# Block-sparse attention and MoE-MLP in one kernel: where the first weight is decoded, in how many steps it is split, and a new order of the work

## The chip, the cores and the metric

The kernel runs on one core of a Trainium2 chip. The metric is the device time of one execution in microseconds (us). A core has TensorE (PE, matrix products), VectorE (DVE), ScalarE (ACT), GpSimd (POOL), SyncE (SP, which here issues nearly all DMAs) and DMA engines. Each engine runs its instructions in the order in which the program queued them and waits on semaphores for the others.

## What is computed

Attention is over 4 batches, 8 heads, 768 tokens and 64 features, in blocks of 32 tokens: a query block sees its neighbours, the first and the last block, and three drawn at random; the first and the last query block see all. Its result x (3072 tokens of 512 features) goes through an MLP.

```python
scores = scale * np.matmul(q, k.transpose(0, 1, 3, 2))    # masked to the blocks above
attn = np.exp(scores - np.max(scores, axis=-1, keepdims=True))
attn = attn / (np.sum(attn, axis=-1, keepdims=True) + 1e-09)
x = np.matmul(attn, v).transpose(0, 2, 1, 3).reshape(B * S, H * D)
h = x @ w_in                                              # 512 x 2048
g = h * np.tanh(np.where(h > 20.0, h, np.log1p(np.exp(np.minimum(h, 20.0)))))
return g @ w_out                                          # 2048 x 512
```

Both weights arrive as 64-bit floats, whose bits the kernel reads as pairs of 32-bit integers.

## The kernel before

**Precision and weights.** x, w_in, g and w_out are held as pairs of half-precision tiles, a high and a low part, and a product is summed from matmuls of parts. Before that, w_in must be made fp32, scaled and split. It comes in eight pieces of 1 MB (`load_i`, tiles `wr`, a ring of three). `add_decode` makes fp32 numbers of a piece by three integer instructions on VectorE (L921, L924, L927); before the change they are written over the place in the constant tile `wi` where the two parts will stand. A Gram matrix of the piece (`add_gram`, PE L365, diagonal on DVE L380) gives a size, from which `add_root` makes a power of two, `ws`, for two pieces at a time (PE `tp_w`, DVE L396, L399, L250). Then `split_i` scales and splits the piece by three instructions: a scaled copy `wt_i` in the ring `raw` (on ACT L975 for five pieces, on POOL L977 for three), the high part, a copy on ACT (L982), and the low part, scaled copy minus high part (POOL L985 for six, DVE L986 for two). w_out follows in sixteen pieces of 512 KB (`wor`, decoded by the same three lines).

**Attention.** 52 jobs of one or two query tiles run in order, thirteen to a batch. A job is S (PE: scores, L650 and L660), `mx` (DVE L703: row maxima), `nb` and `pt` (ACT L716, L729: exponentials), t (PE transposes, L749), `pp` (ACT, DVE: probabilities), O (PE L796, L812), `r` and `xs` (DVE L833 to L848), `tx` (PE L866) and the two parts of x, `xh` (ACT L884) and `xl` (DVE L887). For a job the needed K columns are copied to `kg` (`gather_k`: POOL L588, or ACT L590), and the V rows are fetched from a copy of V in DRAM, `vd`, into `vg` by SP (`gather_v`, L607 to L613). Batch 0 is computed in fp32, so its V is first copied by `copy_v` (L532) and stored by `store_v` (L538).

**MLP.** A tile of 256 tokens is complete after four or five jobs. Then come its h matmuls (`moe_h`, L1065), the function g in the rings `us` and `hs` (three buffers each), and y (`moe_y`, L1125).

**Order.** Every step is a task of the class `Plan` with a planned duration, a `key` (lower goes first among those ready), and buffers of rings that it takes. `emit` queues, over and over, the task that can start first by the plan. `pace` holds S back so that attention is spread over the MLP's matmuls, by the numbers `RES` and `START`, and adds 0.1 us when PE's work changes between S, O and the rest. Where the plan has PE idle for over 0.25 us between 3 and 150 us, `emit` puts in matmuls on a tile of zeros (L900), so many as fit at 0.22 us each. A step that depends on a DMA waits for a semaphore of that DMA; such semaphores are reused, so a DMA's issue can wait for the end of an earlier DMA that had the same one.

## Time and profile before

| what | value |
|---|---|
| device time, median of 3 runs (lowest to highest) | 749.08 us (746.91 to 750.20) |
| the profiled execution's own time | 745.22 us |
| its span | 743.3 us |
| PE busy | 723.2 us, 97% |
| DVE busy | 529.8 us, 71% |
| ACT busy | 541.6 us, 73% |
| POOL busy | 235.9 us, 32% |
| matmuls on zeros (L900) | 136 |

The profile shows one execution. A line is named by its number in the program, a tile by its name in it. "Busy" says how long an engine executed, not whether anything waited for it; that is read from the waits and from the timelines.

### The profile page before, as it was taken

How to read it: one execution, taken by the hardware profiler on the slowest of the kernel's cores; microseconds unless marked ns; L12 is line 12 of the kernel's file. 1: busy time of each engine (PE TensorE's matmuls, PEld its weight loads, DVE VectorE, ACT ScalarE, POOL GpSimd, SP SyncE). 2: the span in 40 equal slices, each digit the busy share in tenths (PEclk: the TensorE clock that was granted, in tenths of full speed). 3: DMA queues.
4: the chain of work that ended last, by engine and by line, in shares of the span. 5: the costliest groups of instructions: out<-in, count | busy, mean ns of one | idle time of the engine just before them, and what ended most of it. 6: DMA issues, size and time to landing. Idle time of an engine off the chain costs nothing.

```text
span 743.3 us, 25914 instructions
## 1 busy us (share of the span) xinstructions
PE 723.2 (97%) x10798; PEld 498.0 (67%) x10798; DVE 529.8 (71%) x1000; ACT 541.6 (73%) x874; POOL 235.9 (32%) x325
## 2 busy tenths in 40 slices
PE   9888898999999999999999999999999999999997
PEld 3555777776676777667677677767767676666653
DVE  3789898788777688888678766789789656334340
ACT  3567787998988777878777877878878766655550
POOL 2263543654416313234324334422154112000000
PEclk9999999999999999999999999999999999999999
DMA  7988878240543563264142651452333343100000
GB/s 269 367 244 254 251 224 263 73 120 29 175 120 86 157 189 116 59 191 114 45 131 70 178 172 59 124 187 67 88 111 87 94 136 80 38 15 15 15 14 29
DMA packets 55897, 93.94 MB, mean 126 GB/s; under 512 B 8036, under 2 KB 18789, under 8 KB 55781
## 3 DMA queue, kind: packets, MB, share of 16 engines
q1 hardware_dynamic: 55584, 92.03, 41.5%
q8 instruction: 85, 1.39, 0.8%
q14 instruction: 32, 0.25, 0.1%
q10 hardware_dynamic: 196, 0.27, 0.1%
HBM read 79.32 MB, written 12.95 MB: 124 GB/s over the span
## 4 chain that ended last, share of the span: by engine, by line
PE 84%; DMA 7%; DVE 6%; ACT 2%; issue 1%; SPq 1%; ACTq 0%; DVEq 0%
PE y L1125 33%; PE h L1065 32%; PE t L749 6%; PE o L812 5%; PE s L660 4%; DMA vg<-vd 3%; DMA wr<-in_moe_w_in_dram 2%; PE tx L866 1%; DMA kt<-in_k_dram 1%; PE o L796 1%; DVE wo L927 1%; DMA raw_q<-in_q_dram 1%; DVE wi L927 1%; DVE wo L924 1%; DMA vd<-z 1%
## 5 line engine op out<-in xcount | busy, mean ns | idle before, releaser
L1065 PE MATMUL h<-xh,wi 128*128 128x256 f16 x1536 | 283.5, 273 | 0.0
L1125 PE MATMUL y<-wo,g 128*128 128x512 f16 x1152 | 276.7, 379 | 0.0
L1065 PEld LDWEIGHTS <-wi 128*128 128x128 f16 x2304 | 223.2, 98 | 47.7 <-issue 1.5
L1065 PE MATMUL h<-xl,wi 128*128 128x256 f16 x768 | 209.7, 273 | 0.0
L1125 PEld LDWEIGHTS <-g 128*128 128x128 f16 x1152 | 111.3, 98 | 100.6 <-issue 1.3
L588 POOL COPY kg<-kt 128x256 f16 (+1 forms) x222 | 105.2, 517 | 186.9 <-PE s L660 154.6
L1074 ACT ACTIVATE hs<-h,gsc 128x512 f32<-128x512 f32 x96 | 65.5, 684 | 59.0 <-PE h L1065 58.7
L729 ACT ACTIVATE pt<-s,nb,ns 128x256 f32<-128x256 f32 (+1 forms) x208 | 104.9, 579 | 3.1 <-DVE nb L718 2.2
L1098 DVE SCALAR_TENSOR_TENSOR hs<-us,hs 128x1024 f32<-128x1024 f32 x48 | 59.7, 1244 | 36.3 <-ACT us L1097 36.0
L1094 POOL TENSOR_TENSOR us<-us 128x1024 f32<-128x1024 f32 x26 | 50.9, 1956 | 85.7 <-DVE us L1092 78.2
L749 PE MATMUL t<-ident,pt 128*128 128x128 f32 x448 | 70.2, 279 | 1.7 <-ACT pt L729 1.1
L769 DVE SCALAR_TENSOR_TENSOR pp<-t,pp 128x512 f16<-128x512 f32 x84 | 57.1, 683 | 17.3 <-ACT pp L766 16.8
L766 ACT ACTIVATE pp<-t 128x512 f16<-128x512 f32 x84 | 49.3, 591 | 21.9 <-PE t L749 21.3
L749 PEld LDWEIGHTS t<-ident,pt 128*128 128x128 f32 x448 | 51.0, 142 | 13.5 <-issue 3.3
L1109 POOL TENSOR_TENSOR g<-hs,g 128x1024 f16<-128x1024 f32 x17 | 38.1, 2239 | 65.8 <-DVE g L1106 30.2
L703 DVE TENSOR_REDUCE mx<-s 128x4 f32<-128x1024 f32 x44 | 53.3, 1212 | 5.9 <-PE s L660 3.1
L1088 ACT ACTIVATE us<-hs,hsc 128x1024 f32<-128x1024 f32 x48 | 55.3, 1151 | 1.3
L1096 ACT ACTIVATE us<-us 128x1024 f32<-128x1024 f32 x48 | 50.8, 1058 | 4.9 <-POOL us L1094 3.9
L1092 DVE TENSOR_SCALAR us<-us 128x1024 f32<-128x1024 f32 x48 | 34.7, 722 | 25.8 <-ACT us L1088 25.6
L1097 ACT ACTIVATE us<-us 128x1024 f32<-128x1024 f32 x48 | 50.8, 1057 | 0.8
L812 PEld LDWEIGHTS <-pp 128*32 128x32 f16 x2952 | 32.5, 97 | 11.4 <-issue 9.7
L1111 DVE TENSOR_TENSOR g<-hs,g 128x1024 f16<-128x1024 f32 x31 | 38.3, 1235 | 2.3 <-ACT g L1104 1.6
(201 smaller groups left out, 855.5 us busy)
## 6 DMA issues: line engine op xcount, KB each, us to landing
vg<-vd SPq DMA_DIRECT2D x304, 65.0 KB, 2.3
vg<-vd SPq DMA_DIRECT2D x80, 195.0 KB, 3.1
wr<-in_moe_w_in_dram SPq DMA_DIRECT2D x8, 1024.0 KB, 9.4
wor<-in_moe_w_out_dram SPq DMA_DIRECT2D x16, 512.0 KB, 5.3
vd<-v SPq DMA_DIRECT2D x12, 520.0 KB, 4.1
raw_v<-in_v_dram SPq DMA_DIRECT2D x12, 512.0 KB, 6.4
...
```

The lines of the kernel that those rows point to most:

```text
L588: nc.gpsimd.tensor_copy(out=dst, in_=src)
L703: nc.vector.tensor_reduce(out=mx.rearrange("p g w -> p (g w)"), in_=tl[ks].rearrange("p g (w k) -> p (g w) k", k=KT), axis=AX.X, op=ALU.max)
L729: ex = lambda o, x, g, w: nc.scalar.activation(out=o, in_=x, func=AF.Exp, bias=nb[:, g, w:w + 1], scale=ns(w)[:, 0:1])
L749: nc.tensor.transpose(t[:, k, g], src, ident)
L769: nc.vector.scalar_tensor_tensor(out=tl["pl", i, j], in0=tl["t", i, j], scalar=PSC, in1=tl["ph", i, j], op0=ALU.mult, op1=ALU.subtract)
L812: nc.tensor.matmul(o[cs, at] if v1 == VW else o[cs, at, 0:v1 - v0], p[:, k, g, cs], x, start=j == 0 and g == 0 and k == 0 and n == 0, stop ...
L1065: nc.tensor.matmul(h[:, f2].rearrange("p (s q) -> p s q", q=BS), wi[:, fp, w, cc, fs], x[:, :, cc], start=f2 == 0 and k == 0, stop=f2 == 1 ...
L1074: nc.scalar.activation(out=tl[kq][:, 2 * (fp % 2):2 * (fp % 2) + 2], in_=tl[kh], func=AF.Copy, scale=gsc[:, fp:fp + 1])
L1088: nc.scalar.activation(out=new(sb, "us", ku, [P, 4, TT]), in_=hs(), func=AF.Exp, scale=hsc[:, b:b + 1])
L1094: add("POOL", 2.0, lambda: nc.gpsimd.tensor_tensor(out=us(), in0=us(), in1=us(), op=ALU.mult), w=[ku], port=True, key=47 + (56 if b == 0 e ...
L1098: add("DVE", 1.32, lambda: nc.vector.scalar_tensor_tensor(out=hs(), in0=us(), scalar=-0.5, in1=hs(), op0=ALU.add, op1=ALU.mult), r=[ku], w ...
L1125: nc.tensor.matmul(tl[ky], tl["g", b, t, k][:, g, f, q], wo[:, fc, w], start=fc == 0 and n == 0, stop=fc == NFC - 1 and n == 2)
```

## The change

1. **Place.** A piece of w_in is decoded into a buffer of the MLP's ring `us` (even pieces) or `hs` (odd ones), named `a`, and no longer into `wi`.
2. **Split.** The high part is one scaled copy of that tile (ACT, all eight), the low part one instruction of VectorE (`a` times scale minus high part, all eight). The scaled copy `wt_i` is gone: 16 instructions stand for 24.
3. **Planned durations** of several tasks are set anew, `pace` counts the 0.1 us only on entering S or O, and its 0.3 us between S and O are gone.
4. **Order.** `RES`, `START` and almost all keys are new, and with them the whole order.

```diff
-    def add_decode(raw, key, dst, dur, cls):
+    def add_decode(raw, key, dst, dur, cls, slot=(), first=None):
...
     def a0_i(k):
-        return wi[:, k].rearrange("p t c f -> p (t c f)").bitcast(F32)
+        return tl["a0", k]
+
+    def at_i(k):
+        ring = ("us", "hs")[k % 2]
+        return [(ring, ("a0", k))], lambda: new(sb, ring, ("a0", k), [P, 4 * TT])
...
-        add_decode(("wr", k), key, lambda: a0_i(k), 1.22, cls)
+        add_decode(("wr", k), key, lambda: a0_i(k), 1.22, cls, *at_i(k))
...
-            if eng == "ACT":
-                nc.scalar.activation(out=t, in_=a0_i(k), func=AF.Copy, scale=sc())
...
-        add("ACT", 1.1, lambda: nc.scalar.activation(out=hi, in_=tl[kt], func=AF.Copy), r=[kt],
...
-        add("POOL", 2.1, lambda: nc.gpsimd.tensor_tensor(out=lo, in0=tl[kt], in1=hi, op=ALU.subtract),
...
+        add("ACT", 1.16, lambda: nc.scalar.activation(out=hi, in_=a0_i(k), func=AF.Copy, scale=sc()), r=[ksc, ("wa", k)],
...
+        add("DVE", 1.27, lambda: nc.vector.scalar_tensor_tensor(out=lo, in0=a0_i(k), scalar=sc(), in1=hi, op0=ALU.mult, op1=ALU.subtract),
+            r=[ksc, ("wa", k), ("wih", k)], w=[("wi", k)], use=[ka], port=True, key=cls + 12)
...
-    RES, START = 152, [75, 143, 351, 1, 289, 59, 444, 40, 4, 303, 106, 133, 87, 206, 53, 166, 65, 18]
+    RES, START = 180, [97, 103, 720, 17, 173, 0, 747, 0, 13, 609, 79, 124, 130, 10, 140, 182, 96, 42]
...
-                shape, at["shape"] = 0.1 * (now != at["shape"]), now
+                shape, at["shape"] = 0.1 * (now not in (None, at["shape"])), now
...
-        if kind in ("S", "O") and at["last"] in ("S", "O") and kind != at["last"]:
-            late = max(late, 0.3)
```

Other planned durations of the diff: `gather_k` on POOL 1.3 to 1.5, on ACT 1.6 or 1.9 to 1.0; `sums` 1.28 to 1.06; S of the later batches 0.7 to 0.78; the exponentials 1.15 to 1.03; t 0.48 to 0.44; `tx` 0.25 to 0.22.

In the new order PE's work is the same but for the zeros (165 matmuls for 136, six of the added ones among later h blocks); it enters S or O from other work 103 times instead of 115, and S and O stand directly side by side 15 times instead of 2. Of the K gathers 99 copies stand on ACT instead of 42, and 165 on POOL instead of 222, in 32 groups on ACT instead of 14.

**SP queue, the first loads.** `kt`, `q` and `raw_v` are K, Q and V of batch 0, `wr` are pieces of w_in. Before:

```order
L416 DMA kt_123<-in_k_dram 128x4x768
L416 DMA q_0_157<-in_q_dram 128x4x256
L434 DMA raw_v_0_161<-in_v_dram 128x2x512
L434 DMA raw_v_1_163<-in_v_dram 128x2x512
L434 DMA raw_v_2_165<-in_v_dram 128x2x512
L416 DMA q_1_167<-in_q_dram 128x4x256
L913 DMA wr_169<-in_moe_w_in_dram 128x4x512
L913 DMA wr_171<-in_moe_w_in_dram 128x4x512
L913 DMA wr_173<-in_moe_w_in_dram 128x4x512
```

and now:

```order
L416 DMA kt_123<-in_k_dram 128x4x768
L416 DMA q_0_157<-in_q_dram 128x4x256
L416 DMA q_1_161<-in_q_dram 128x4x256
L913 DMA wr_163<-in_moe_w_in_dram 128x4x512
L913 DMA wr_165<-in_moe_w_in_dram 128x4x512
L913 DMA wr_167<-in_moe_w_in_dram 128x4x512
L434 DMA raw_v_0_169<-in_v_dram 128x2x512
L434 DMA raw_v_1_171<-in_v_dram 128x2x512
L434 DMA raw_v_2_173<-in_v_dram 128x2x512
L913 DMA wr_316<-in_moe_w_in_dram 128x4x512
L913 DMA wr_361<-in_moe_w_in_dram 128x4x512
```

Three pieces of w_in and a second tile of Q went ahead of V.

**SP queue, around the first V gathers.** `vd` is V's copy in DRAM; the rows of L557 fetch the global blocks, those of L607 to L613 the other blocks of jobs 1 and 2. Before, from the fourth piece of w_in on:

```order
L913 DMA wr_378<-in_moe_w_in_dram 128x4x512
L913 DMA wr_469<-in_moe_w_in_dram 128x4x512
L557 DMA vg_111<-vd_60 32x520 x2
...
L913 DMA wr_557<-in_moe_w_in_dram 128x4x512
L607 DMA vg_111<-vd_60 64x520
L610 DMA vg_111<-vd_60 32x520
L567 TENSOR_LOAD offv
...
L613 DMA vg_111<-vd_60 32x520
```

and now:

```order
L913 DMA wr_442<-in_moe_w_in_dram 128x4x512
L538 DMA vd_60<-v_2_159 128x2x520
L913 DMA wr_673<-in_moe_w_in_dram 128x4x512
L557 DMA vg_111<-vd_60 32x520 x2
...
L913 DMA wr_768<-in_moe_w_in_dram 128x4x512
L607 DMA vg_111<-vd_60 64x520
L610 DMA vg_111<-vd_60 32x520
L567 TENSOR_LOAD offv
L613 ISA
L613 DMA vg_111<-vd_60 32x520
```

The seventh and the eighth piece (`wr_673`, `wr_768`) went ahead of job 1's gathers, which stand behind the eighth; before, the seventh and the eighth stood among the gathers of jobs 1 to 3.

**VectorE, around the fifth piece of w_in.** Names `wr`, `a` and `wi` as above (`a_4` is the fifth piece, with the number of the buffer behind it), `gram_wi` a Gram diagonal, `mx` a job's maxima. Before, from the last step of the fourth piece (`wr_378`), a low part ahead of it, to the last step of the fifth (`wr_469`):

```order
L986 TENSOR_TENSOR wi<-wt_i_566,wi 128x1024
L927 SCALAR_TENSOR_TENSOR wi<-wr_378,wi 128x1024
L921 TENSOR_SCALAR wi<-wr_469 128x1024
L921 TENSOR_SCALAR wi<-wr_557 128x1024
L924 SCALAR_TENSOR_TENSOR wi<-wr_469,wi 128x1024
L703 TENSOR_REDUCE mx_797<-s_700 128x4
L380 SCALAR_TENSOR_TENSOR gram_wi_736,wq_568<-gram_wi_736,ident 128x128
L924 SCALAR_TENSOR_TENSOR wi<-wr_557,wi 128x1024
L396 TENSOR_SCALAR iv_i<-tp_w_828 128x2
L399 TENSOR_SCALAR iv_i<-iv_i 128x2
L250 TENSOR_SCALAR ws_850<-iv_i 128x2
L927 SCALAR_TENSOR_TENSOR wi<-wr_469,wi 128x1024
```

and now:

```order
L929 SCALAR_TENSOR_TENSOR a_4_588<-wr_361,a_4_588 128x1024
L703 TENSOR_REDUCE mx_766<-s_709 128x4
L981 SCALAR_TENSOR_TENSOR wi<-a_2_347,ws_700,wi 128x1024
L380 SCALAR_TENSOR_TENSOR gram_wi_770,wq_816<-gram_wi_770,ident 128x128
L981 SCALAR_TENSOR_TENSOR wi<-a_3_467,ws_700,wi 128x1024
L926 SCALAR_TENSOR_TENSOR a_5_704<-wr_442,a_5_704 128x1024
L923 TENSOR_SCALAR a_6_856<-wr_673 128x1024
L923 TENSOR_SCALAR a_7_858<-wr_768 128x1024
L929 SCALAR_TENSOR_TENSOR a_5_704<-wr_442,a_5_704 128x1024
L926 SCALAR_TENSOR_TENSOR a_6_856<-wr_673,a_6_856 128x1024
L380 SCALAR_TENSOR_TENSOR gram_wi_904,wq_816<-gram_wi_904,ident 128x128
```

Where one old low part stood ahead of the fifth piece's steps, the low parts of two pieces stand directly behind the fifth piece's last step, and the first steps of the seventh and the eighth piece follow before the sixth piece is decoded.

## Rows read from the trace of the kernel before

**Rows 1.** Windows of busy time, whole core: stretch, its length, busy us of each engine (x instructions), granted TensorE clock (1.00 is full), mean share of the DMA engines, GB/s.
```profile
0.00:83.42 83.42, 71.00 (x1207) 42.65 (x1208) 63.01 (x125) 45.90 (x93) 33.71 (x55) 0.98 0.87 276
83.42:160.00 76.58, 73.39 (x1268) 57.07 (x1263) 66.80 (x133) 68.45 (x111) 37.05 (x35) 1.00 0.66 199
160.00:700.00 540.00, 539.48 (x8109) 376.60 (x8107) 387.49 (x731) 411.29 (x655) 165.11 (x236) 1.00 0.35 101
700.00:743.30 43.30, 39.33 (x224) 21.69 (x222) 12.52 (x13) 15.96 (x18) 0.00 (x0) 1.00 0.05 20
```

**Rows 2.** The same view for the filler matmuls of line 900 alone.
```profile
0.00:83.42 83.42, 34.50 (x136) 13.32 (x136) 0.98 0.87 276
```

**Rows 3.** TensorE's waits over the span: waiting line, what ended the wait, us in total, times, longest us.
```profile
PE o L796 <- DMA vg<-vd: 3.5, 6, 1.2
PE gram_wi L365 <- DVE wi L927: 3.2, 3, 2.3
...
PE s L650 <- POOL kg L588: 0.7, 1, 0.7
```

**Rows 4.** Chain of waits from 12 to 84 us: start us, us, what held it.
```profile
13.47 8.52 DMA wr<-in_moe_w_in_dram
...
38.30 5.43 DMA vg<-vd
```

**Rows 5.** VectorE's timeline: start us, us, line, operation, out<-in, in brackets the idle time before and what ended it.
```profile
10.65 0.81 DVE L532 COPY v<-raw_v 128x1024 f32<-128x1024 f32 x1 [0.82 <-DMA raw_v<-in_v_dram]
...
15.19 0.16 DVE L701 TENSOR_TENSOR mx<-mx 128x2 f32<-128x2 f32 x1
...
22.01 0.69 DVE L921 TENSOR_SCALAR wi<-wr 128x1024 int32<-128x1024 int32 x1 [4.98 <-DMA wr<-in_moe_w_in_dram]
...
82.35 1.23 DVE L703 TENSOR_REDUCE mx<-s 128x4 f32<-128x1024 f32 x1 [1.72 <-PE s L650]
83.49 0.68 DVE L927 SCALAR_TENSOR_TENSOR wo<-wor,wo 128x512 int32<-128x512 int32 x1
```

**Rows 6.** Waits of the SP queue up to 26 us, columns as in rows 3.
```profile
SPq L434 <- DMA q<-in_q_dram: 6.3, 1, 6.3
...
SPq L434 <- DMA vd<-z: 3.0, 1, 3.0
```

**Rows 7.** Windows of busy time in steps of 2 us, columns as in rows 1.
```profile
12.00:14.00 2.00, 2.00 (x36) 0.73 (x36) 0.73 (x1) 1.62 (x4) 1.04 (x1) 1.00 0.34 11
...
20.00:22.00 2.00, 1.88 (x15) 1.58 (x14) 0.00 (x0) 0.72 (x2) 0.00 (x0) 1.00 1.05 388
```

**Rows 8.** VectorE's groups by shape from 160 to 600 us: line, operation, out<-in, shape xcount, busy us, mean ns of one, idle before.
```profile
L503 DVE SCALAR_TENSOR_TENSOR q<-raw_q,sc_q,q 128x1024 f16<-128x1024 f32 x8 | 10.4, 1300 | 1.2 <-DMA vg<-vd 0.7 <-ACT q L499 0.5
```

**Rows 9.** The same for 15.4 to 112 us.
```profile
L927 DVE SCALAR_TENSOR_TENSOR wo<-wor,wo 128x512 int32<-128x512 int32 x13 | 10.2, 797 | 0.0
...
L921 DVE TENSOR_SCALAR wo<-wor 128x512 int32<-128x512 int32 x14 | 5.9, 427 | 0.0
L986 DVE TENSOR_TENSOR wi<-wt_i,wi 128x1024 f16<-128x1024 f32 x2 | 3.6, 1776 | 0.1
```

**Rows 10.** VectorE's timeline, columns as in rows 5.
```profile
47.40 0.17 DVE L399 TENSOR_SCALAR iv_i<-iv_i 128x2 int32<-128x2 int32 x1
...
47.68 1.22 DVE L927 SCALAR_TENSOR_TENSOR wi<-wr,wi 128x1024 int32<-128x1024 int32 x1
...
54.63 1.59 DVE L399 TENSOR_SCALAR iv_i<-iv_i 128x2 int32<-128x2 int32 x1
...
60.40 3.15 DVE L927 SCALAR_TENSOR_TENSOR wi<-wr,wi 128x1024 int32<-128x1024 int32 x1
...
76.82 3.81 DVE L924 SCALAR_TENSOR_TENSOR wo<-wor,wo 128x512 int32<-128x512 int32 x3
```

**Rows 11.** GpSimd's timeline, columns as in rows 5.
```profile
51.81 4.39 POOL L985 TENSOR_TENSOR wi<-wt_i,wi 128x1024 f16<-128x1024 f32 x2 [1.92 <-ACT wi L982]
...
60.18 2.29 POOL L985 TENSOR_TENSOR wi<-wt_i,wi 128x1024 f16<-128x1024 f32 x1 [2.57 <-ACT wi L982]
```

**Rows 12.** VectorE's waits from 15 to 95 us, columns as in rows 3.
```profile
DVE gram_wi L380 <- PE gram_wi L365: 1.4, 1, 1.4
```

**Rows 13.** The tile view of the weight ring, its line on the loads from issue to landing.
```profile
DMA to landing us min/median/max: 7.0/9.4/12.8
```

**Rows 14.** TensorE's timeline, columns as in rows 5.
```profile
43.87 0.91 PE L796 MATMUL o<-vg,pp 128*32 128x65 f32 x32 [0.16 <-DMA vg<-vd]
...
165.12 1.46 PE L1125 MATMUL y<-wo,g 128*128 128x512 f16 x6
166.51 1.17 PE L660 MATMUL s<-kt,q 64*32 64x512 f16 x48
...
175.61 1.45 PE L1125 MATMUL y<-wo,g 128*128 128x512 f16 x6
176.90 0.27 PE L1065 MATMUL h<-xh,wi 128*128 128x256 f16 x1
```

**Rows 15.** ScalarE's timeline, columns as in rows 5.
```profile
525.39 1.02 ACT L590 ACTIVATE kg<-kt 128x256 f16 x3 [0.96 <-POOL kg L588]
```

**Rows 16.** The SP queue's timeline, columns as in rows 5.
```profile
33.57 0.61 SPq L607 DMA_DIRECT2D vg<-vd  x1
```

More of the change, by code (lines that the diff above doesn't have):

```diff
@@ L403, in add_root @@
     def add_root(key, ss, fn, r, after, w, new, cls, n=1, apart=False):
-        add("PE", 0.3 * n, lambda: root_pe(key, ss(), apart), r=r, w=[key], new=[("t", key)], key=cls + 56, lat=0.3)
-        add("DVE", 0.65, fn, port=2, r=[key, *after], w=w, new=new, key=cls + 3)
+        add("PE", 0.3 * n, lambda: root_pe(key, ss(), apart), r=r, w=[key], new=[("t", key)], key=cls + 5, lat=0.3)
+        add("DVE", 0.65, fn, port=2, r=[key, *after], w=w, new=new, key=cls - 69)
     def load32(what, j):
@@ L437, in load @@
         add("SP", 0.5 * n, fn, r=after, w=keys,
-            new=[(ring, key) for key in keys], key=(-5 if b == 0 else 0) + (0 if b == 0 else 59), lat=1.8,
+            new=[(ring, key) for key in keys], key=(-5 if b == 0 else 0) + (18 if b == 0 else 106), lat=1.8,
             kind=("dma", 1.5 * n, n))
@@ L448, in fn @@
             squares(tl["raw", what, b, j], tl[key][:, k:k + 1])
-        add("ACT", 1.28, fn, r=[("raw", what, b, j)], w=[key], new=[(f"ss{what}", key)] if first else (), key=cls + 47 + (19 if b == 0 else 19))
+        add("ACT", 1.06, fn, r=[("raw", what, b, j)], w=[key], new=[(f"ss{what}", key)] if first else (), key=cls + 47 + (4 if b == 0 else -13))
     def scales(b, what, j, cls):
@@ L510, in parts @@
         if what == "v":
-            add("POOL", 0.5, ends, w=[("ends",) + key], r=[kr], new=[("raw", key)], use=[key], key=cls + 9)
+            add("POOL", 0.5, ends, w=[("ends",) + key], r=[kr], new=[("raw", key)], use=[key], key=cls + 6)
         kh = ("hi",) + key
@@ L514, in parts @@
             new={"k": [("kt", kt)] if first else [], "q": [("q", key)], "v": []}[what],
[L515 to L516 removed]
+            use=use + ([key] if what != "k" else []), key=cls + 9)
+        add("DVE", 1.27, lo, port=True, r=[kr, ks, kh], w=[key, ("done",) + key], use=use, key=cls - 73)
     def copy_v(j):
@@ L532, in fn @@
                 (nc.vector if eng == "DVE" else nc.gpsimd).tensor_copy(out=dst, in_=src)
-        add("POOL", 0.3, ends, w=[("ends",) + key], new=[("raw", key)], use=[key], key=-2)
-        add("DVE", 0.8, lambda: fn("DVE"), r=[kr, ("ends",) + key], w=[key], use=[key], key=ATV + 94, port=True,
+        add("POOL", 0.3, ends, w=[("ends",) + key], new=[("raw", key)], use=[key], key=-58)
+        add("DVE", 0.8, lambda: fn("DVE"), r=[kr, ("ends",) + key], w=[key], use=[key], key=ATV, port=True,
             also=[("ACT", 1.16, lambda: fn("ACT")), ("POOL", 2.0, lambda: fn("POOL"))])
@@ L720, in attend @@
         add("ACT", 0.25 * len(wq), lambda: nb_fn("ACT"), r=[kmx] + NS, w=[("nb", i)],
-            new=[("nb", ("nb", i))], key=45.5 + (21 if b == 0 else -20), also=[("DVE", 0.35 * len(wq), lambda: nb_fn("DVE"))])
+            new=[("nb", ("nb", i))], key=45.5 + (44 if b == 0 else -18), also=[("DVE", 0.35 * len(wq), lambda: nb_fn("DVE"))])
         def ex_fn(n):
@@ L738, in attend @@
         for n in range(2):
-            add("ACT", 1.7 if dense and n == 0 else 1.15, lambda n=n: ex_fn(n),
+            add("ACT", 1.7 if dense and n == 0 else 1.03, lambda n=n: ex_fn(n),
                 r=[kmx, ("nb", i), ks] + (k2 if dense else []) + NS,
-                w=[("p", i, n)], new=[("pt", k) for k in kps] if n == 0 else (), use=kps, key=-1.5 + (-3 if b == 0 else 54))
+                w=[("p", i, n)], new=[("pt", k) for k in kps] if n == 0 else (), use=kps, key=-1.5 + (36 if b == 0 else 95))
         def t_fn(j):
@@ L914, in load_w @@
         tl[key] = raw.rearrange("p (f two) -> p f two", two=2)
-    def add_decode(raw, key, dst, dur, cls):
+    def add_decode(raw, key, dst, dur, cls, slot=(), first=None):
         def fn(n):
+            if n == 0 and first:
+                first()
             a0i, lo_w, hi_w = dst().bitcast(I32), tl[raw][..., 0], tl[raw][..., 1]
@@ L930, in add_decode @@
             add("DVE", dur * (0.55, 1, 1)[n], lambda n=n: fn(n), port=True, r=[raw],
-                w=[key] + ([("dec", raw[1])] if n == 2 and raw[0] == "wr" else []), key=cls + 26)
+                w=[key] + ([("dec", raw[1])] if n == 2 and raw[0] == "wr" else []), new=slot if n == 0 else (), use=[k for _, k in slot], key=cls + 94)
     def a0_i(k):
-        return wi[:, k].rearrange("p t c f -> p (t c f)").bitcast(F32)
+        return tl["a0", k]
+    def at_i(k):
+        ring = ("us", "hs")[k % 2]
+        return [(ring, ("a0", k))], lambda: new(sb, ring, ("a0", k), [P, 4 * TT])
     def load_i(k):
@@ L993, in load_o @@
         add("SP", 0.5, lambda: load_w(sb, raw, "raw", w_out.rearrange("(c p) f -> p c f", p=P)[:, fc], a0_o(fc)),
-            r=after, w=[raw, ("wo", fc)], new=[("raw", raw)], key=-6, lat=1.8, kind=("dma", 1.5, 1))
+            r=after, w=[raw, ("wo", fc)], new=[("raw", raw)], key=92, lat=1.8, kind=("dma", 1.5, 1))
     def piece_o(fc, cls):
@@ L1035, in fn @@
             nc.vector.tensor_scalar(out=gsc, in0=iv_i, scalar1=rg, scalar2=-2.0 * GSC, op0=ALU.mult, op1=ALU.mult)
-        add("DVE", 0.7, fn, r=[("iv", k) for k in range(0, NFP, 2)], w=["gsc"], key=27)
+        add("DVE", 0.7, fn, r=[("iv", k) for k in range(0, NFP, 2)], w=["gsc"], key=28)
     def scales_b(b):
@@ L1183, in attn_mish_kernel @@
     add("ACT", 1.0, lambda: which(new), w=["off", "z"],
-        new=[("raw", ("z",))], key=-6, lat=6.0)
+        new=[("raw", ("z",))], key=7, lat=6.0)
     globals_(0)
```

118 lines of the change are left out of this document (54 added, 64 removed).

## The prediction

> **What bounds the kernel now.** I read the windows of busy time first. TensorE is the bound: from 160 to 700 us it is busy 539.48 of 540.00 us, and VectorE, ScalarE and GpSimd have room there [rows 1]. Nothing on them can shorten that stretch; only a different list of matmuls, or a gap that opens, changes it. What can be won lies before 160 us and in the last 43 us, where 3.97 us are idle. Up to 83.42 us (the start of the third block of h matmuls) TensorE is busy 71.00 us, of which 34.50 us are the 136 filler matmuls on zeros of L900 [rows 1, 2], so only 36.5 us of the 83.42 are work. From there to 160 us 3.19 us are idle [rows 1].
>
> What holds the start is read from the waits and the chain of waits. TensorE waits for V gathers and for decoded weights [rows 3], and the chain goes through the first weight load (8.52 us) and a V gather (5.43 us) [rows 4]. On VectorE's timeline a wait of 4.98 us for that load stands before the first decode at 22.01, and nearly no gap after it until 82.35, where it waits 1.72 us for S [rows 5]. So up to there the sum of VectorE's list, with the moment of the first load, sets when the first token tile is complete. The sum below follows that list.
>
> **The change, part by part.** Counting matmuls in both orders, the changed kernel's first h block stands where the kernel before stood at 83.42 us: one S more (1.2 us), two transposes more, twelve weight Grams more, two h blocks of 1.3 us less; by the durations they cancel to 0.1 us. So I ask when VectorE has delivered the last low part of x ahead of that block. The same stretch of the list ended before at 83.49 + 0.68 = 84.17 [rows 5].
>
> 1. First load. Before, three V loads and one of Q were issued ahead of the first weight load, and the SP queue stood still for 6.3 and 3.0 us on DMAs asked for earlier [rows 6]; from 12 to 14 us the DMA engines moved 11 GB/s [rows 7]. Now the weights stand ahead of V. The first V copy could run at 10.65 [rows 5], so 2.5 MB had landed; one MB more at the 388 GB/s of a full stretch [rows 7] takes 2.6 us: an estimate of 13.3 us. VectorE is then still at job 0's maxima, which end at 15.35 [rows 5]. The decode starts there and not at 22.01: -6.66 us. (The V copies, two of them on VectorE before, go to ScalarE; one lay in this very gap, the other in idle time.)
> 2. Eight low parts in one pass each. That operation and shape took 1300 ns for Q [rows 8]: +10.40 us. Two old low parts go: -3.55 us [rows 9].
> 3. Ahead of the last low part of x now stand three more w_out first passes (427 ns) and two more second or third passes (797 ns): +2.9 us [rows 9].
> 4. GpSimd's big passes over w_in go. While one ran, a decode pass took 3.15 us instead of 1.22, a 2-element operation 1.59 instead of 0.17, three w_out passes 3.81 instead of 1.92 (three of the 0.68 of the row at 83.49, less their overlaps) [rows 5, 10], and GpSimd's rows have a pass of L985 running over each of the first two [rows 11]. That is 1.93 + 1.42 + 1.89 = -5.2 us. The Trainium skill ("SBUF — State Buffer", section "SBUF: two separate sides") calls the port pair that the two engines share an exclusive lock for whole instructions, which a VectorE pass with two SBUF inputs takes too, against a GpSimd operation that reads SBUF. The rows agree for the first half: 3.15 us is 1.22 plus most of GpSimd's 2.29. By the other half the eight new passes hold GpSimd's gathers; that is rival D.
> 5. Waits. Before, 1.7 us for S and 1.4 us for a Gram [rows 12] are in the 84.17. New: the eighth weight load waits for the fifth piece's decode (ring of three). Before, that decode ended 33.55 us after the maxima (15.35 to 48.90 [rows 5, 10]), 6.66 of it the gap of step 1. The new list has two low parts more (2.6), and one old low part (1.8), one decode pass (1.2) and one maximum (1.2) less: 25.3, so 40.6 us. The load is issued 0.4 later and takes 9.4 us (7.0 to 12.8) [rows 13]: landed at 50.4. VectorE asks for it six passes after the fifth piece, at about 46.7: a wait of 3.7 us (1.3 to 7.1). Against the 3.1 us that I let go: +0.6 (-1.8 to +4.0).
>
> The list: 84.17 - 6.66 + 10.40 - 3.55 + 2.9 - 5.2 + 0.6 = 82.7, and half a microsecond for TensorE to start on it: 83.2 against 83.42, **-0.2 us**. Its bounds: -3.1 (short load, and 1.1 us more of smaller stretches gone) to +5.6 (long load, and only the largest stretch gone).
>
> 6. After that. The changed kernel has six filler matmuls among its later h blocks, where there were none: 6 x 254 ns (34.50 / 136 [rows 2]) = 1.5 us if they come on top, or they stand in part of the 3.19 us that was idle anyway, half of which could go (-1.6). Nothing separates these: **0**, with both ends kept.
> 7. Entries into attention work. In the gapless part a y block lasts 1.39 us before an S and 1.29 before an h [rows 14], 0.10 more. The order has 103 entries into S or O from other work, it had 115: 12 x 0.10 = -1.2 us. Direct switches between O and S, 15 where there were 2, aren't counted as entries; if each costs as much, the term is nothing. I take **-1.1 us** (0 to -1.3).
> 8. K gathers: 57 copies move from GpSimd to ScalarE, in 18 more groups. Three took 1.02 us with 0.96 idle ahead [rows 15]: 18 x 1.98 = 36 us of ScalarE's time, if all lie in the steady part 447 of 540 us instead of 411.29 [rows 1]. TensorE's queue of h and y blocks covers that: **0**; without this cover it is rival C. ScalarE also loses five scaling copies, and its three stay hidden.
>
> Sum: -0.2 + 0 - 1.1 = -1.3 us, between -6.0 and +7.1. The profiled execution's span of 743.3 (its own time is 745.22) becomes 742.0. That execution is 3.86 us under the median of 749.08, so the forecast is **747.8 us**, no change that a measurement can tell: about 0.5%, 3.75 us, is what one can.
>
> **Rivals.** A, faster: VectorE's list runs without the new wait, because the DMA queue has lost its hole at 12 to 14 us and the eighth load lands in the short 7.0 us; later idle time shrinks too. For it: loads stand first in the queue. Against: V's loads, its stores and the gathers now press on the same stretch, with a DMA share of 0.87 before [rows 1]. Low ends throughout: -3.1 - 1.6 - 1.3 = -6.0, so 743.1.
>
> B, slower: job 1's V gathers. They stood between the sixth and the seventh weight load, issued from 33.57 on [rows 16]; now they stand behind the eighth, that is behind the fifth piece's decode, 40.6 us by step 5, and the second of job 2's is issued on a semaphore that the eighth load frees. Job 1's O used to start at 43.87 [rows 14]; the new order has it after the fifth Gram, so until a decode end of about 43 the gathers (4 to 5 us) cost nothing; beyond that every microsecond is one of the whole. It decides if VectorE begins at 22.01 as before: the decode then ends at 47.3, 4.3 past that point, and the same delay takes step 1's 6.66 us back. The two are one delay and the longer counts: -1.3 + 6.7 = +5.4, so 754.5.
>
> C, slower: ScalarE gives exponentials or K gathers late and gaps open after 160 us. S waited once 0.7 us for a gather [rows 3]; if half the 18 new groups did so it is +6.3: 754.1. Against: 83% busy still leaves 93 us.
>
> D, slower: what GpSimd's passes did to VectorE [rows 10, 11] the eight low parts, also long passes with two SBUF inputs, do to GpSimd's K gathers for the next job. If each makes S wait the 0.7 us that it once waited for a gather [rows 3], that is +5.6: 753.4. Against: GpSimd loses nine long passes of its own in that stretch.
>
> **How the numbers follow.** Forecast (within 0.5%) 0.40; A 0.36; B 0.11, C 0.08, D 0.05. I give A much because the sum is below zero already, two of its bounds lie on that side, and step 1 rests on a row. Faster 0.36, same 0.40, slower 0.24. The range takes in A's time with a little below, and all three slow rivals: 741.5 to 755.5; the forecast's own is 745.3 to 752.8.
>
> **What would show it.** Step 1: the first decode pass at about 15.4 us. Step 4: no decode pass over 1.5 us before the first h. Step 5: a wait of some 4 us for a w_in load at the start of the eighth piece. First h block at 83 us, with TensorE's real work up to it 36.5 us. Step 6: idle and zeros from there to 160 us together near 3.2. Step 7: 160 to 700 us still gapless, its list 1.1 us shorter. Wrong it is if the decode starts late (B), if O waits for gathers longer than the 3.5 us of rows 3, or if ScalarE's new groups leave S waiting.

## The result, and the profile after

| | kernel before | changed kernel |
|---|---|---|
| median, same chip, 8 runs each | 748.49 us (745.50 to 752.44) | 755.88 us (752.42 to 759.31) |
| ratio, 95% interval | 1 | 1.0082 (1.0056 to 1.0108): slower by 0.8% |
| profiled execution, own time and span | 745.22, 743.3 us | 759.04, 757.2 us |

Forecast were 747.8 us and no change. The measured time lies 0.4 us above the range and on the slow side. The two profiled executions differ by 13.9 us, the medians by 7.4: the profile of after is 3.2 us above its median, that of before 3.3 below its own. They also differ in the granted TensorE clock, averaged over the span: 0.991 in the changed kernel's, 0.998 in the other. The eight executions of the changed kernel have 0.994 on average, and those of the kernel before that were timed beside the experiments 0.993. So part of the 13.9 us can be the clock's, while the loss in the medians is not. From the profiles I read where time goes, and from medians and ratios how much of it.

The windows of the changed kernel, whole core, columns as in [rows 1]:

```profile
0.00:83.42 83.42, 73.21 (x1130) 41.53 (x1134) 60.78 (x125) 45.50 (x94) 11.12 (x41) 0.94 0.82 270
83.42:160.00 76.58, 69.72 (x1117) 52.57 (x1106) 61.67 (x120) 57.04 (x96) 25.95 (x25) 0.98 0.61 165
160.00:700.00 540.00, 538.11 (x8278) 378.92 (x8279) 389.74 (x743) 421.43 (x707) 168.45 (x202) 1.00 0.37 107
```

The same for the zeros of L900 alone, beside [rows 2]:

```profile
0.00:83.42 83.42, 41.45 (x157) 15.62 (x157) 0.94 0.82 270
83.42:160.00 76.58, 3.17 (x8) 0.86 (x8) 0.98 0.61 165
```

Up to 83.42 us TensorE is busier than before (73.21 for 71.00 us), but zeros are 41.45 of it: 31.8 us of work for 36.5, and the granted clock fell to 0.94. The steady part is nearly gapless still. To see where work falls behind, I counted each kernel's matmuls without the zeros at the price that their rows have at full clock (an h matmul 0.11 us, one of y 0.22) and noted when the sum reached a value. The sum is an estimate: in the gapless part attention's price is too high (250 us of work pass in 233.5 us), so only the lags are read:

| work done, us | 20 | 25 | 30 | 35 | 45 | 50 | 60 | 150 | 400 | 680 |
|---|---|---|---|---|---|---|---|---|---|---|
| before, at us | 60.0 | 69.5 | 74.7 | 83.2 | 93.8 | 98.6 | 110.6 | 201.5 | 435.0 | 701.5 |
| after, at us | 58.3 | 66.8 | 82.5 | 88.4 | 100.9 | 112.3 | 123.0 | 215.2 | 450.6 | 715.8 |
| lag | -1.7 | -2.7 | 7.8 | 5.2 | 7.1 | 13.7 | 12.5 | 13.7 | 15.6 | 14.2 |

The change is ahead until 66.8 us and then loses twice: 10.5 us up to 82.5 us and 6.6 between 100.9 and 112.3. After that the lag hardly grows. TensorE's waits in the changed kernel, columns as in [rows 3]:

```profile
PE o L796 <- DMA vg<-vd: 8.1, 10, 2.1
PE s L650 <- issue: 2.2, 1, 2.2
```

The waits for w_in's Grams (3.2 us in rows 3) are gone; O's waits for V gathers went from 3.5 to 8.1 us. TensorE's timeline, columns as in [rows 14]:

```profile
47.74 1.00 PE L796 MATMUL o<-vg,pp 128*32 128x65 f32 x32 [1.18 <-DMA vg<-vd]
...
68.72 1.13 PE L796 MATMUL o<-vg,pp 128*32 128x65 f32 x32 [1.56 <-DMA vg<-vd]
...
73.89 0.76 PE L650 MATMUL s<-kg,q 64*32 64x160 f32 x9 [2.18 <-issue]
74.58 5.27 PE L900 MATMUL zeros<-z 128*128 128x512 f16 x12
79.67 0.40 PE L866 MATMUL tx<-ident,xs 128*128 128x128 f32 x2
...
88.40 0.27 PE L1061 MATMUL h<-xh,wi 128*128 128x256 f16 x1
...
105.14 0.32 PE L796 MATMUL o<-vg,pp 128*32 128x65 f32 x8 [2.05 <-DMA vg<-vd]
```

At 68.72 an O block has waited 1.56 us. Then TensorE stands still for 2.18 us in the middle of an S, for nothing that the profile names ("issue"), and the twelve zeros behind it take 5.27 us. Three windows of 2 us there, columns as in rows 1:

```profile
68.00:70.00 2.00, 1.15 (x48) 0.87 (x56) 2.00 (x3) 0.11 (x1) 0.00 (x0) 0.86 0.71 162
...
72.00:74.00 2.00, 0.12 (x5) 0.11 (x8) 0.00 (x0) 0.07 (x1) 0.00 (x0) 0.50 1.01 389
...
78.00:80.00 2.00, 2.00 (x7) 0.81 (x6) 0.61 (x2) 0.24 (x1) 0.00 (x0) 0.58 0.07 26
```

The granted clock falls behind O's wait and ahead of the stall (0.86 from 68 to 70 us). Where TensorE stands it is at 0.50, the lower of its two levels, and the DMA engines are full (share 1.01, 389 GB/s). At 78 us the DMA engines are nearly idle. Why shows on the SP queue's timeline:

```profile
59.10 2.34 SPq L913 DMA_DIRECT2D wor<-in_moe_w_out_dram  x3
...
68.34 1.30 SPq L913 DMA_DIRECT2D wor<-in_moe_w_out_dram  x3
...
73.07 0.36 SPq L913 DMA_DIRECT2D wor<-in_moe_w_out_dram  x1
80.61 0.32 SPq L607 DMA_DIRECT2D vg<-vd  x1
```

and before:

```profile
65.73 2.59 SPq L913 DMA_DIRECT2D wor<-in_moe_w_out_dram  x4
```

The w_out loads wait, by the program, for the seventh piece of w_in to be decoded. VectorE is there earlier now: its last pass over that piece ends at 53.85 us (52.61 + 1.24, shown below) and not at 63.55 [rows 10]. So in the new order the first three loads of 512 KB stand behind five groups of V gathers and no longer behind eight, and go out at 59.10 and not at 65.73 us. From 73.43 on the queue stands still, waiting for an O block that must free a `vg` buffer, of which there are two; that O stands on TensorE behind the stall and the twelve zeros and starts at 80.00. The SP queue's waits from 55 to 115 us, columns as in [rows 6]:

```profile
SPq L607 <- PE o L796: 7.8, 3, 7.2
SPq L613 <- DMA wor<-in_moe_w_out_dram: 5.8, 5, 2.1
```

and before:

```profile
SPq L607 <- PE o L796: 8.5, 5, 4.2
...
SPq L613 <- DMA wor<-in_moe_w_out_dram: 1.6, 1, 1.6
```

The queue waited as long for O blocks before, but in shorter pieces. New are the one long stand and the second row: a gather whose semaphore a w_out load had is issued only when that load has landed. Gather, O and next gather form a ring, so a w_out load that delays a gather can delay O, and O's delay then leaves the queue empty. That is read from the waits; no run had another number of buffers. The median landing times from 55 to 112 us in the view of DMA issues (x issues, KB each, us to landing), after:

```profile
wor<-in_moe_w_out_dram SPq DMA_DIRECT2D x16, 512.0 KB, 6.8
vg<-vd SPq DMA_DIRECT2D x12, 195.0 KB, 6.6
vg<-vd SPq DMA_DIRECT2D x34, 65.0 KB, 5.0
```

and before:

```profile
vg<-vd SPq DMA_DIRECT2D x36, 65.0 KB, 3.6
vg<-vd SPq DMA_DIRECT2D x11, 195.0 KB, 4.6
```

A gather takes 1.4 to 2.0 us longer. The chain of waits, which had a gather of 5.43 us in [rows 4], has two longer ones, one in each of the two losses:

```profile
62.10 6.49 DMA vg<-vd
...
101.41 8.82 DMA vg<-vd
```

VectorE meanwhile did what was forecast; its timeline, beside [rows 5] and [rows 10]:

```profile
14.40 0.69 DVE L923 TENSOR_SCALAR a<-wr 128x1024 int32<-128x1024 int32 x1
...
39.07 1.22 DVE L929 SCALAR_TENSOR_TENSOR a<-wr,a 128x1024 int32<-128x1024 int32 x1
...
41.48 1.27 DVE L981 SCALAR_TENSOR_TENSOR wi<-a,ws,wi 128x1024 f16<-128x1024 f32 x1
...
46.75 0.69 DVE L923 TENSOR_SCALAR a<-wr 128x1024 int32<-128x1024 int32 x1 [0.85 <-DMA wr<-in_moe_w_in_dram]
...
52.61 1.24 DVE L929 SCALAR_TENSOR_TENSOR a<-wr,a 128x1024 int32<-128x1024 int32 x1
...
74.72 1.22 DVE L703 TENSOR_REDUCE mx<-s 128x4 f32<-128x1024 f32 x1 [4.30 <-PE s L650]
```

The last row is the turn: VectorE, which held the start before, now waits 4.30 us for TensorE's S.

### The profile page after: what moved, and what is told of

Its sections match the earlier page's. It is cut to its first block, busy times and chain, and to the rows that moved or that the text cites. A ratio compares the mean times of both kernels' runs of the same rounds, so it can differ in the third digit from the quotient of the medians.

```text
span 757.2 us, 25968 instructions
## 1 busy us (share of the span) xinstructions
PE 734.6 (97%) x10827; PEld 504.1 (67%) x10827; DVE 528.0 (70%) x1003; ACT 548.2 (72%) x921; POOL 205.5 (27%) x267
## 4 chain that ended last, share of the span: by engine, by line
PE 77%; DMA 8%; ACT 6%; DVE 6%; issue 2%; SPq 0%; ACTq 0%; POOL 0%; DVEq 0%; POOLq 0%
PE y L1121 30%; PE h L1061 28%; PE t L749 5%; PE o L812 4%; PE s L660 4%; DMA vg<-vd 3%; DMA wor<-in_moe_w_out_dram 2%; DMA raw_v<-in_v_dram 1%; PE s L650 1%; PE tx L866 1%; DMA q<-in_q_dram 1%; PE zeros L900 1%; PE o L796 1%; ACT pt L729 1%; DVE mx L703 1%
## 5 line engine op out<-in xcount | busy, mean ns | idle before, releaser
L588 POOL COPY kg<-kt 128x256 f16 (+1 forms) x165 | 78.5, 517 | 180.0 <-PE s L660 106.4
L1090 POOL TENSOR_TENSOR us<-us 128x1024 f32<-128x1024 f32 x30 | 59.4, 1979 | 125.9 <-DVE us L1088 125.9
L769 DVE SCALAR_TENSOR_TENSOR pp<-t,pp 128x512 f16<-128x512 f32 x84 | 56.3, 682 | 15.8 <-ACT pp L766 15.4
L1105 POOL TENSOR_TENSOR g<-hs,g 128x1024 f16<-128x1024 f32 x20 | 44.5, 2227 | 73.1 <-DVE g L1102 27.7
L590 ACT ACTIVATE kg<-kt 128x256 f16 (+1 forms) x99 | 30.9, 376 | 29.9 <-PE t L749 6.5
L900 PE MATMUL zeros<-z 128*128 128x512 f16 x165 | 44.6, 413 | 1.7 <-POOL z L895 1.7
```

The lines of the kernel that those rows point to most:

```text
L588: nc.gpsimd.tensor_copy(out=dst, in_=src)
L769: nc.vector.scalar_tensor_tensor(out=tl["pl", i, j], in0=tl["t", i, j], scalar=PSC, in1=tl["ph", i, j], op0=ALU.mult, op1=ALU.subtract)
L900: nc.tensor.matmul(spare[0].rearrange("p (n q) -> p n q", q=P), z16, z16.unsqueeze(1).to_broadcast([P, 4, P]), start=True, stop=True)
L1090: add("POOL", 2.0, lambda: nc.gpsimd.tensor_tensor(out=us(), in0=us(), in1=us(), op=ALU.mult), w=[ku], port=True, key=47 + (61 if b == 0 e ...
```

## The experiments

The theories: the order costs by way of V gathers and w_out loads; the split itself costs; the zeros and the low clock cost. Ratios are against the kernel before, timed beside each version.

**The split or the order.** `e1_code` puts the decode into the rings and the two-step split into the kernel before and leaves its keys.

```diff
-        add_decode(("wr", k), key, lambda: a0_i(k), 1.22, cls)
+        add_decode(("wr", k), key, lambda: a0_i(k), 1.22, cls, *at_i(k))
...
-        add("POOL", 2.1, lambda: nc.gpsimd.tensor_tensor(out=lo, in0=tl[kt], in1=hi, op=ALU.subtract),
```

> The kernel before with the ring decode and the two-step split alone; keys, durations and pace are those of before. Theory T (w_out loads start as soon as the seventh piece of w_in is decoded, and since VectorE gets there earlier they go in front of V gathers, O waits, TensorE's clock falls): twelve w_out loads now stand ahead of the gathers of job 3 on the SP queue, 12 x 1.35 us (512 KB at 388 GB/s) of transfer, so clearly slower than before, 757 to 766 us, with V waits of O over 8 us. Theory S (the split itself costs, eight more long passes on VectorE): 753 to 757, with V waits as before. If the split is a gain by itself: under 747.

790.34 us, 1.0545 (1.0509 to 1.0581). The planner made another order of it, with twelve w_out loads and their decoding ahead of the first token tile; its two longest waits of TensorE are on decoding and on `hs`:

```profile
PE gram_wi L365 <- DVE a L929: 5.2, 4, 2.2
PE h L1061 <- ACT hs L1070: 4.4, 1, 4.4
```

So it tests an order that nobody tuned, and tells nothing of the split. `e2_order` is the reverse, planned anew too: the changed kernel's keys, durations and pacing with the old decode and three-step split.

```diff
-        add_decode(("wr", k), key, lambda: a0_i(k), 1.22, cls, *at_i(k))
+        add_decode(("wr", k), key, lambda: a0_i(k), 1.22, cls)
...
+        add("POOL", 2.1, lambda: nc.gpsimd.tensor_tensor(out=lo, in0=tl[kt], in1=hi, op=ALU.subtract),
```

> The changed kernel's keys, durations and pace with the old decode in place and the old three-step split. Theory T: the order is what costs; the w_out loads again start right behind the seventh piece, in front of gathers: 752 to 758. Theory S: the order is good and the split bad: at most 748.

760.94 us, 1.0157 (1.0122 to 1.0192): the new order costs without the new split, more than with it. `e16_split_only` holds the order fixed: the kernel before, instruction by instruction where it was, with the new decode and split alone.

```diff
-        add("ACT", 1.1, lambda: nc.scalar.activation(out=hi, in_=tl[kt], func=AF.Copy), r=[kt],
+        add("ACT", 1.1, hi_fn, r=[kt], w=[("wi", k), ("wih", k)], key=cls + 37, also=[("DVE", 0.8, hi_fn)])
...
+            nc.vector.scalar_tensor_tensor(out=lo, in0=a0_i(k), scalar=sc(), in1=hi, op0=ALU.mult, op1=ALU.subtract)
```

> The kernel before in its own exact order on every engine, with the new split alone: the first weight is copied into the rings that the MLP uses later, the scaled copy is dropped, the high part is one scaled copy where the high part stood, the low part one instruction of VectorE at the place of the old low part. Theory Q (the order of the weight loads and gathers on SP's queue is what costs, not the split): VectorE gets 10.4 us of low parts and loses 3.55 of old ones and some 5.2 of stretched passes, +1.6 us on its list, and the gathers and w_out loads stay where the kernel before has them: 745 to 752, ratio 0.995 to 1.003, and the O blocks wait for V gathers as long as in the kernel before (3.5 us in all) give or take 1.5. Theory S (the split itself costs, VectorE's longer list): 753 or more, with TensorE waiting for VectorE or for decoded weights before 84 us.

750.24 us, 1.0008 (0.9983 to 1.0034): no difference. Its VectorE timeline has the short decode pass and the low part as in the changed kernel, and O waits 5.0 us in all, for 3.5 before and 8.1 in the changed kernel:

```profile
62.93 1.22 DVE L929 SCALAR_TENSOR_TENSOR a<-wr,a 128x1024 int32<-128x1024 int32 x1
64.06 1.28 DVE L978 SCALAR_TENSOR_TENSOR wi<-a,ws,wi 128x1024 f16<-128x1024 f32 x1
```

```profile
PE o L796 <- DMA vg<-vd: 5.0, 6, 1.7
```

In the old order the split is free within 0.3%. With the new keys it helps, as far as two orders that were planned apart can be compared (1.0157 without, 1.0082 with it). So the loss is the order's.

**The zeros.** `e3_no12` leaves out the twelve zeros of 74.58 us.

```diff
-            if t.eng == "PE" and self.zeros and self.FROM < start < self.TILL and idle > 0.25:
+            if t.eng == "PE" and self.zeros and self.FROM < start < self.TILL and idle > 0.25 and t.kind != ("X", 3):
```

> The changed kernel without the 12 filler matmuls ahead of job 3's tx (74.58 to 79.67 us in the profile after). Theory F (fillers at the half clock hold up tx, O and the next gathers): their end came 2.8 us after the data (76.9 by VectorE's xs), and all behind moves: 752 to 753.5, 2.5 to 4 us less than the changed kernel. Theory T: the stretch waits for V gathers behind w_out loads anyway, so within 1.5 us of the changed kernel (755.9).

759.93 us, 1.0140 (1.0104 to 1.0177), above the changed kernel's 1.0082, at a mean granted clock of 0.989 for 0.994. `e4_moved12` has them ahead of the second half of that job's O, `e8_more12` has twelve in both places.

```diff
+            if t.kind == ("O", 3) and any(x.kind == ("O", 3) for x in self.order):
+                self.zeros(12)
```

> The changed kernel with the same 12 filler matmuls ahead of the second half of job 3's O, where TensorE waited 1.56 us for V with some 1.8 us idle shortly before, and not behind the S that follows. Theory F: the clock stays at full level through that S (no stretch under 0.9 from 66 to 82 us), 750 to 753. Theory T: idle time for V stays what it is and the clock falls somewhere behind it; within 1.5 us of the changed kernel or of e3.

> The changed kernel with 12 filler matmuls more, ahead of the second half of job 3's O, and all others kept. Theory C (TensorE's clock falls in the idle time there and the work behind runs at the half clock, which is most of the loss between 66 and 82 us): the clock holds, 751 to 753.5. Theory T (the crowd of transfers holds V and TensorE's next instructions, the clock is only a sign of it): 755.5 to 758, the fillers themselves 0 to 3 us.

755.06 us, 1.0076 (1.0047 to 1.0105), and 754.38 us, 1.0055 (1.0028 to 1.0082): as the changed kernel. In the profile of `e8_more12` the clock stays at 1.00 from 60 to 80 us, both runs of twelve zeros take 2.75 us, and its lag is 4.5 us at 30 us of work and 9.5 at 50 all the same. So the low clock is not what the medians lose, as its averages in the section on the result say too (0.994 and 0.993). It may be the 4.7 us by which the profile of after lags further than this one at its end (14.2 and 9.5): their granted clocks are 0.991 and 0.998.

**Single moves.** `e7_wor_later` holds all w_out loads until job 5's S is there (planned anew), `e9_wor_one` puts three of them behind the next group of gathers and keeps every other place, `e12_v_first` undoes what rival B spoke of: the eighth piece of w_in goes behind job 1's gathers.

```diff
-        if i == 1:
-            LOADO, ATO, ATP = [("dec", 6)], -3.0, -24.0
+        if i == 5:
+            LOADO, ATO, ATP = [("dec", 6), ("begun", 5)], -3.0, -24.0
```

> The changed kernel with the w_out loads held until job 5's S has been planned: the first three go behind one more group of gathers, the next three behind one more again; what the plan puts elsewhere moves a little. Theory T: fewer V waits of O (under 7 us) and 751 to 754. Theory R: 755 to 757.

```diff
+    MOVED = (3, 4, 5)
...
+        k = now.index(("wor", fc))
+        x = log.pop(k)
...
+        g = next(n for n in range(k, len(log)) if now[n] and now[n][0] == "gv")
...
+        log.insert(g + 1, x)
```

> The changed kernel in exactly its order on every engine, but for three w_out loads (the fourth to the sixth) that go behind the next group of V gathers on the SP queue. Theory T in its narrow form (w_out loads directly ahead of a gather group cost what they take, 3 x 1.35 us): 752 to 754.5. Theory T in its wide form (it is the whole crowd of w_out bytes between 59 and 110 us, not the place of one group): 755 to 757.

```diff
+    k = where.index(("wr", 7))
+    last = log.pop(k)
+    g = next(n for n in range(k, len(log)) if tags()[n] == ("gv", 1))
+    log.insert(g + 1, last)
```

> The changed kernel in exactly its order on every engine, but for the eighth w_in load, which goes behind the gathers of job 1 on the SP queue (rival B of the prediction undone). Theory B: job 1's O starts before 46.8 us instead of 47.74, its gathers no longer wait for the fifth piece, and the loop of gathers and O's that follows is earlier: 751 to 754. If the place of these gathers isn't what costs: 755 to 757, with job 1's O at the same time or the time lost again by 70 us.

762.64 us, 1.0167 (1.0139 to 1.0196); 757.83 us, 1.0096 (1.0064 to 1.0129); 760.36 us, 1.0138 (1.0097 to 1.0178). None gains. In `e12_v_first` the first w_out load goes out at 65.15 us, about as late as in the kernel before (65.73), but still behind five groups of gathers, so a later start alone is no cure. The Grams wait for the late piece instead, and O still waits 7.1 us (its line numbers are one higher):

```profile
PE o L797 <- DMA vg<-vd: 7.1, 8, 3.0
PE gram_wi L365 <- DVE a L930: 5.6, 1, 5.6
```

`e10_pace` gives the changed kernel the old pacing, `e11_wfirst` gives the kernel before the first loads of w_in ahead of V, both planned anew.

```diff
-    RES, START = 180, [97, 103, 720, 17, 173, 0, 747, 0, 13, 609, 79, 124, 130, 10, 140, 182, 96, 42]
+    RES, START = 152, [75, 143, 351, 1, 289, 59, 444, 40, 4, 303, 106, 133, 87, 206, 53, 166, 65, 18]
```

> The changed kernel with RES, START and pace of the kernel before; all keys and durations stay, the order follows from them. Here four w_out loads stand ahead of the gathers two groups earlier still. Theory T: slower than the changed kernel, 757 to 763. If RES, START and pace are what cost: 749 to 752.

```diff
-            key=-5, lat=1.8, kind=("dma", 4.4 if what == "k" else 1.5, 1))
+            key=-25, lat=1.8, kind=("dma", 4.4 if what == "k" else 1.5, 1))
...
-             new=[(ring, key) for key in keys], key=(-5 if b == 0 else 0) + (0 if b == 0 else 59), lat=1.8,
+             new=[(ring, key) for key in keys], key=(-5 if b == 0 else 0) + (18 if b == 0 else 59), lat=1.8,
```

> The kernel before with two keys changed: w_in's first three pieces and Q's second tile are loaded ahead of V, as in the change. The first decode moves from 22.0 to about 15 us, and the plan then puts five w_out loads ahead of four more groups of gathers. Theory T: what VectorE gains comes back as a crowd of transfers: 751 to 758, with first h later than 77.6 us or V waits of O over 6 us. If the early w_in is a gain by itself: 742 to 746.

776.04 us, 1.0331 (1.0286 to 1.0377), and 777.71 us, 1.0347 (1.0307 to 1.0387). Both planned the w_out loads earlier (the second after four groups of gathers) and lose 14.5 and 8.7 us of work by 60 us of it; both lose more again later (32.6 and 36.0 at 680), which I didn't follow up. Together with `e1_code` they say that a part of this tuned order can't be exchanged alone, and no more.

**Bytes and gathers.** `e5_quarter_after` and `e6_quarter_before` load a quarter of each w_out piece and decode it four times over, so the time of VectorE stays and three quarters of the bytes go (w_out's values are then other ones). `e13_quarter6` does so for the first six pieces alone.

```diff
-        add("SP", 0.5, lambda: load_w(sb, raw, "raw", w_out.rearrange("(c p) f -> p c f", p=P)[:, fc], a0_o(fc)),
+        add("SP", 0.5, lambda: load_w(sb, raw, "raw", w_out.rearrange("(c p) f -> p c f", p=P)[:, fc, 0:DM // 2], a0_o(fc)),
```

> The changed kernel with each w_out load cut to its first quarter (128 KB of 512, and the decode reads that quarter four times), so three quarters of w_out are left out; every instruction, its place and its waits are the same. Theory T (w_out loads ahead of V gathers on the same queue hold O up): V waits of O fall from 8.1 to under 4 us and the time to 747 to 750, most of what the change cost. Theory R (the new order itself waits, for VectorE's and ScalarE's steps, and the clock follows): 753 or more.

> The kernel before with the same cut of the w_out loads, as the reference for e5. Theory T: it gains little, 746 to 748.5, since its loads stand behind eight groups of gathers; e5 less e6 is at most 2.5 us. Theory R: e5 less e6 stays at 5 us or more.

> The changed kernel with only the first six w_out loads cut to a quarter (they are issued from 59 to 70 us), the other ten whole; of those six pieces three quarters are left out. Theory T says that these bytes make the loss between 66 and 82 us and the other ten the one between 100 and 112 us: the first loss gone (25 to 30 us of TensorE's work take 7 to 9 us, not 15.7), the second there, 750 to 752. If it is one loss that any of the bytes triggers: 754 or more, or 748 or less.

747.03 us, 0.9950 (0.9929 to 0.9971); 745.58 us, 0.9942 (0.9918 to 0.9966); 751.23 us, 1.0004 (0.9981 to 1.0026). The changed kernel gains 9 us from the missing bytes, the kernel before 4.5, and 1.5 us are left between them. Part of both gains can be the clock's, which is 0.999 and 0.997 on average here. With the first six pieces short, the first loss goes (lag 0.2 us at 35 us of work) and the second stays (5.8 at 50). O's waits are no measure of the loss: they hardly fell in `e5_quarter_after` (7.4 us), and in `e6_quarter_before` they are 6.3 us for 3.5, in a faster kernel. The stall on "issue" is gone in `e5_quarter_after`.

`e14_nov_after` and `e15_nov_before` fetch batch 0's V rows for the first two groups only; the later O blocks of that batch read what lies in the buffers.

```diff
+            if exact(b) and su["ng"] >= NVG:
+                return
```

> The changed kernel without the V gathers of batch 0 behind job 1 (their O's read the V rows that are in the buffers), so that O never waits for V; w_out's and the next batch's loads are then issued in one row. Theory V (the loss is O's waits for gathers): 742 to 747, no worse than e15 by over 2 us. Theory I (w_out's bytes hold TensorE's own instructions and VectorE's data up, and the clock falls): 750 or more, with waits of TensorE on nothing that the profile shows over 3 us.

> The kernel before with the same gathers left out, as the reference for e14. Theory V: 740 to 746, a gain of 4 to 8 us, since O waited 3.5 us for V. Theory I: 747 to 751.

744.94 us, 0.9908 (0.9873 to 0.9943), and 747.16 us, 0.9948 (0.9926 to 0.9970). Without these gathers nothing of the loss is left in the medians. The changed kernel even leads by 2.2 us, but at a mean granted clock of 0.998 for 0.994; the two profiled executions, both at 0.998, took 745.27 and 743.23 us. What is left of O's wait in the changed kernel (lines two higher):

```profile
PE o L798 <- DMA vg<-vd: 1.2, 1, 1.2
```

**One queue or shared engines.** `e17_wor_act_after` and `e18_wor_act_before` issue the w_out loads from ScalarE's DMA queue, so that no gather stands behind one in its queue. In the changed kernel the first load then goes out at 55.73 us, earlier still.

```diff
-        nc.sync.dma_start(out=raw.rearrange("p (c f) -> p c f", c=w.shape[1]) if len(w.shape) == 3 else raw, in_=w)
+        (nc.scalar if tag == "raw" else nc.sync).dma_start(out=raw.rearrange("p (c f) -> p c f", c=w.shape[1]) if len(w.shape) == 3 else raw, in_=w)
```

> The changed kernel with the w_out loads issued from ScalarE's DMA queue instead of SyncE's; every order on TensorE and VectorE is as in the changed kernel. Theory Q1 (gathers stand behind w_out loads in one queue): the V gathers land in 4.0 to 5.0 us again, waits of O for gathers fall under 4 us in all, 748 to 752. Theory Q2 (all queues share the 16 DMA engines, and it is the bytes that slow a gather, whichever queue they come from): waits of O stay at 7 us or more, 754 to 759.

> The kernel before with its w_out loads on ScalarE's DMA queue, the control of the run on the changed kernel. Theory Q1: its O blocks wait less for V gathers (3.5 us in the trace before), 744 to 748. Theory Q2: no change, 748 to 752.

758.49 us, 1.0118 (1.0081 to 1.0154), and 747.88 us, 0.9977 (0.9947 to 1.0006). No help for the changed kernel, none that can be told for the kernel before. In the former O waits longer than in any other run:

```profile
PE o L796 <- DMA vg<-vd: 13.3, 8, 3.0
```

Gathers of 65 KB landed after 4.4 us there, for 5.0 in the changed kernel and 3.6 before. So taking the loads out of the gathers' queue does not win the time back: gathers and loads share the DMA engines. The Trainium skill says so ("DMA: Bandwidth & Descriptors", section "Issuing engines are not separate DMA queues"), and these two runs agree. This kernel has no stall on "issue" in that stretch and is no faster, so the loss doesn't need the stall.

No version that does the whole work was measurably faster than the kernel before.

## Why the prediction was wrong, point by point

- **What holds the start.** "So up to there the sum of VectorE's list, with the moment of the first load, sets when the first token tile is complete" fits the kernel before, where that list has nearly no gap. For the changed kernel it is the step that failed: the list's own passes came out near the forecast, and something else became the later one. The last low part of x ahead of the block was done at 87.3 us (86.84 + 0.48) for 82.7 forecast, and VectorE had waited 5.2 us for S in all, where I let such waits go. First h block: 88.40 us for 83.2. I followed the weights through the queue and never asked what an earlier decode triggers: the w_out loads, which go out 6.6 us earlier into batch 0's gathers. With three quarters of w_out's bytes away the first h block stands at 82.80 us (`e5_quarter_after`), where the list has it. `e5_quarter_after` and `e14_nov_after`, each beside the kernel before with the same part left out, show that those bytes and those gathers are the cause together; either one away, and the loss is gone to within some 2 us. By which step a late gather becomes so long a delay is read from the waits and not shown by a run.
- **Step 1**, first decode at 15.35 us: 14.40, right. **Step 2**, 1.30 us per low part: 1.27 to 1.28, right. **Step 3**: the same number of passes, but ahead of that block they waited 2.2 us (1.62 and 0.56) for w_out pieces that landed late; no term had that.
- **Step 4**, GpSimd's stretches gone: right, no decode pass of w_in took over 1.24 us, where one of rows 10 took 3.15. The other half of the rule that I weighed there (the Trainium skill, "SBUF — State Buffer", section "SBUF: two separate sides") cost TensorE nothing here: S waited for no GpSimd gather, so rival D did not occur.
- **Step 5**: the fifth piece was decoded at 40.29 us (40.6 forecast), but the wait for the eighth was 0.85 and not 3.7 us. The term that was mis-sized is the load: issued at 40.32 us, it landed at 46.73, after 6.4 us for 9.4.
- **Step 6**, nothing lost after the first block: wrong in size. From 83.42 to 160 us 6.86 us are idle and 3.17 go to zeros, 10.0 together where 3.2 were forecast. It is the second loss, and O waits for gathers in it too: the one at 105.14 waits 2.05 us for a gather that was issued at 98.43 and landed at 105.01, after 6.6 us. The gather of 8.82 us is one for the next O.
- **Step 7**, -1.1 us in the steady part: not seen. The lag went from 13.7 to 14.2 us between 150 and 680 us of work, while TensorE idled 1.89 us for 0.52. The entries may have given 0.9 that the idle time took; nothing here separates the two.
- **Step 8** and rival C: ScalarE worked 421.43 us in the steady part (447 forecast), and no waits of note followed.
- **Rival B** named the right transfers and the wrong place. Job 1's O came 4 us later (47.74), with a wait of 1.18, and the kernel was still ahead by 2.7 us at 25 us of work; undoing it (`e12_v_first`) did not help. **Rival A**, faster: VectorE did decode earlier, but no run that does the whole work shows a gain in time from it. With the gathers gone the changed kernel is 4.8 us ahead of the kernel before at 35 us of work, and the kernel before without them about as far.
- **The sign** that was given for being wrong, O waiting over 3.5 us for gathers, came (8.1 us), though the sum of these waits is no measure of the loss.
- **The range** was cut on the slow side by rivals that priced one delay each. Here two came, 10.5 and 6.6 us in the profile.

**Open.** Which part of the order would mend it: three single moves did not. Also what the stall on "issue" is. A transfer of 16 KB on a queue that the profile calls "instruction" runs from 71.4 to 72.6 us, at the start of the stall of 71.70 to 73.89, while the DMA engines are full. In nine of the traces there are ten stalls of 1.4 us or more before 90 us, and each has such a transfer beginning in it or at most 1 us ahead; but these transfers come every five to twelve us, also where nothing stalls. That speaks for instructions that come late, but no run singled it out, and the kernel before has such a stall of 2.0 us too.
